# Attention into a soft mixture of experts: score tiles of one head's keys instead of two heads' halves, V single buffered, and a new hand-written order

## The chip, the cores and the metric

The kernel runs on one core of a Trainium2 chip. The core has five engines with a queue of instructions each: PE (matrix products, with weight loads that run ahead of them), DVE (element-wise work), ACT (functions such as tanh and exp), POOL (general work, and here the issue of the casting transfers) and SP (here only the issue of transfers). An engine works through its own queue in order and waits on semaphores for the others; transfers run on 16 DMA engines.

The metric is the device time of one launch in microseconds; the time of a version is the median over its runs. Times of instructions come from one profiled execution.

## The reference

```python
# q, k, v: (8, 12, 448, 64), cap = 30
scores = q @ k^T / sqrt(64)
scores = cap * tanh(scores / cap)
attn   = softmax(scores)                   # over the keys
x      = (attn @ v) as 3584 tokens x 768   # 12 heads side by side

logits = x @ phi                           # 768 x 32: 8 experts, 4 slots each
slots  = softmax(logits over the tokens)^T @ x
h      = relu(slots[e] @ w1[e])            # 768 -> 1024, for each expert
out_s  = h @ w2[e]                         # 1024 -> 768
out    = softmax(logits over the slots) @ out_s
```

Attention is most of the work: 96 heads (8 batches of 12) of 448 queries and 448 keys. The expert part reads 25 MB of `w1` and as much of `w2` in float32, cast to bfloat16 on the way.

## The kernel before

**Tiles.** Four heads make a quad (24 of them), two heads a pair `pr` (48). In a quad, the pair `h` of Q and K is turned by PE (`transp`, L337) so that partition 64 h + d holds dimension d; 128 columns hold 64 keys of each of the pair's two heads, for each of seven column groups `c`. A score tile is one `c` of one pair: 128 partitions (64 keys of head 0 above 64 keys of head 1) by 448 queries. `qk_chunk` (L368) makes three tiles, each from two 64x64 products, and the order of the tiles alternates between the two pairs of a quad (`turn`, L169). There are 336 tiles, 112 chunks, and 56 groups of six tiles.

**Softcap and softmax.** ACT takes tanh of a chunk out of PSUM into float16 (`tanh_chunk`, L380). The exponential of a group is then made either by ACT in one instruction (`exp_chunk`, L392) or by DVE in eight instructions, a bit trick with a cubic polynomial (`poly_exp`, L402, steps at L410 to L419). Sixteen groups go to DVE.

**V products.** `pv_mms` (L422) takes the exponentials as weights, 128 queries at a time, against `vbd`, in which the two heads' V stand block by block: 130 columns, 64 of V and one of ones for each head, with zeros where the other head's keys are. The last 64 queries (the tail) are done as two 64x64 products, one for each head. Reciprocal and product on DVE normalise (L444, L448), PE turns the result for the logits (L485), and per batch there follow logits, slot sums and the turned weights of the tokens.

**Loads.** Q and K come through POOL with a cast to bfloat16 (`load`, L251), each into a buffer that the turn two quads before has released. V comes through SP in float32, into two buffers (`load_v`, L259), and POOL casts it into `vbd` (`vcast`, L351). The weights come through POOL between them (`M` in the order): `w1` stays, 13 of the 16 parts of `w2` are parked in DRAM as bfloat16 and are read back when attention releases its memory (L766 to L772), three as whole parts and ten as halves; three parts stay on chip.

**The order.** The stage is written out by hand in `PROGRAM` (L183): `T` tanh of a chunk, `Q` its scores, `p` one of the eight DVE steps of a group, `E` an ACT exponential, `A`/`B`/`t`/`u` the V products of a pair, `r`/`m` its normalisation, `K`/`J` and `k`/`j` turn and copy of K and Q, `X`/`y`/`x` the turn of the output, `L`/`e`/`S`/`s`/`R`/`c`/`W`/`w` the batch work, `M` a weight load, and `G`, `F`, `N` products without use, which keep PE from idling. Each engine meets its instructions in that order. Six groups' buffers `ex` lie in attention's memory, two more (`guests`) in buffers that later take parts of `w2`, and so do `xf` and `xp`, the working buffers of the DVE steps.

**The end.** The last pair, the logits and the slot sums follow by hand; then layer 1, layer 2 for one half of the columns, the first output tiles, layer 2 for the other half, and the output (11 MB).

Of the kernel before, what the change touches and what calls it, by code (L numbers as in the profile page):

```python
# [9 lines left out]
F32 = mybir.dt.float32  # L10
BF16 = mybir.dt.bfloat16
# [27 lines left out]
def kernel(  # L39
# [28 lines left out]
    KEPT = 1 + NGU  # L68
    WHOLE = 3
    EARLY2 = 2  # L70
# [29 lines left out]
    consts.tile([P, 192], BF16, name="pad")  # L100
# [3 lines left out]
    def unit(shape, dt, name):  # L104
        return wts.tile(shape, dt, name=name, tag="w2u", bufs=KEPT + 2)

# [31 lines left out]
    late = len(w2_parts) - NGU  # L138
    w2_kept = w2_parts[:KEPT - NGU] + w2_parts[late:]
    w2_spilled = [(n0, None) for n0 in w2_parts[KEPT - NGU:KEPT - NGU + WHOLE]]  # L140
    w2_spilled += [(n0, half) for half in range(2) for n0 in w2_parts[KEPT - NGU + WHOLE:late]]

# [10 lines left out]

    att = ExitStack()
    ld = att.enter_context(tc.tile_pool(name="ld", bufs=1))
    homes = {}
    for nm in ("qk0", "ldv0", "ex4", "qk1", "ex2", "ldv1", "vb0", "ex1", "ex3", "vb1", "ex5", "ex0"):
        homes[nm] = att.enter_context(tc.tile_pool(name=nm, bufs=1))
# [3 lines left out]
    ldv = [homes["ldv0"], homes["ldv1"]]  # L162
# [21 lines left out]
T0.2 V0.0 V0.1 V1.0 V1.1 T1 Q2 N1.0 T2.1 p0.0 Q3 N4.0 p0.1 T3 p0.2 K1.1 E1 J1.0 k1 j1 Q4 p0.3 Q5  # L184
T4.3 N4.0 p0.4 M0 T5 Q6 p0.5 J2.0 K2.1 T6.4 Q7 j2 T7 k2 Q8 p0.6 N1.0 T8.6 Q9 J3.1 p3.0 T9 Q10 p0.7
K3.0 M1 T10.0 p3.1 Q11 j3 T11 p3.2 A0.1 k3 B0 E2 p3.3 t0 Q12 u0 Q13 A1.0 r0 p3.4 t1 T12.2 B1 m0 u1
M2 p3.5 T13 Q14 J4.1 T14.7 r1 j4 Q15 m1 T15 p3.6 Q16 A2.1 E4 t2 p7.0 K4.0 F7 p3.7 k4 M3 B2 T16.5
p7.1 Q17 X0.0 p7.2 E5 y0 Q18 u2 G9.18 r2 x0 m2 J5.0 p7.3 A3.1 T17 t3 B3 T18.1 p7.4 u3 Q19 M4 r3
G6.19 j5 E6 m3 p7.5 A4.1 Q20 T19 K5.0 p7.6 t4 B4 T20.3 Q21 p9.0 u4 G7.21 E8 r4 m4 M5 k5 A5.1 p7.7
X1.0 t5 p9.1 Q22 T21 B5 p9.2 y1 u5 T22.4 Q23 r5 m5 x1 T23 Q24 X2.1 y2 T24.6 Q25 x2 p9.3 M6 L0.1 T25  # L190
K6.0 k6 e0 E10 J6.1 p9.4 A6.0 j6 Q26 p9.5 t6 Q27 T26.2 B6 u6 p9.6 K7.1 T27 Q28 M7 E12 r6 k7 Q29 m6
G6.29 p13.0 A7.0 p9.7 J7.1 T28.0 t7 p13.1 B7 u7 E11 Q30 r7 m7 G6.30 j7 S0.0 p13.2 M8 A8.1 T29 s0
p13.3 R0.0 T30.7 Q31 t8 c0 B8 p13.4 T31 u8 A9.0 r8 m8 E14 p13.5 X3.1 B9 t9 Q32 u9 Q33 M9 r9 y3 m9
T32.5 G8.33 x3 p13.6 T33 Q34 J8.0 T34.3 A10.1 j8 p16.0 t10 K8.0 E15 p13.7 Q35 B10 k8 u10 Q36 r10
p16.1 M10 A11.0 T35 p16.2 t11 T36.4 Q37 B11 m10 T37 u11 Q38 r11 m11 K9.1 E17 k9 Q39 p16.3 A12.0 J9.1
M11 B12 j9 T38.6 p16.4 X4.1 y4 T39 x4 Q40 p16.5 X5.1 y5 T40.1 Q41 t12 u12 r12 T41 m12 Q42 x5 K10.0
p16.6 T42.2 L1.1 M12 Q43 e1 E18 k10 S1.1 p16.7 A13.0 p20.0 t13 s1 E19 p20.1 J10.1 B13 j10 u13 p20.2
A14.1 r13 T43 Q44 m13 t14 M13 p20.3 R1.0 T44.7 Q45 B14 p20.4 T45 u14 Q46 r14 c1 m14 T46.0 Q47 K11.0
J11.1 T47 k11 j11 A15.0 E22 p20.5 t15 B15 M14 X6.1 Q48 p20.6 u15 Q49 T48.5 y6 x6 T49 p20.7 A16.1 t16
r15 E21 B16 p24.0 u16 Q50 m15 r16 X7.0 m16 M15 Q51 T50.3 y7 A17.1 x7 p24.1 B17 T51 Q52 p24.2 t17 u17  # L200
J12.0 T52.4 r17 Q53 m17 j12 W0.1 E25 w0 K12.0 A18.1 k12 p24.3 X8.0 M16 y8 Q54 T53 B18 x8 t18 T54.6
p24.4 Q55 u18 J13.0 r18 m18 T55 Q56 L2.1 j13 T56.1 p24.5 Q57 K13.0 e2 E23 S2.1 k13 M17 p24.6 A19.0
t19 T57 p27.0 B19 Q58 s2 p24.7 u19 E26 A20.1 r19 B20 m19 t20 p27.1 R2.0 Q59 c2 T58.0 u20 p27.2 N2.0
r20 M18 T59 m20 Q60 p27.3 A21.1 T60.2 Q61 K14.0 p27.4 T61 Q62 k14 p27.5 T62.7 Q63 B21 T63 J14.0 t21
j14 Q64 E28 p27.6 M19 Q65 X9.0 y9 u21 G6.65 r21 x9 m21 T64.5 A22.0 p27.7 K15.1 T65 p31.0 M20 t22 Q66
k15 E29 p31.1 X10.1 B22 p31.2 y10 u22 Q67 r22 G6.67 x10 T66.3 M21 m22 A23.1 p31.3 T67 J15.0 B23 Q68
j15 E30 t23 u23 p31.4 Q69 A24.0 r23 M22 m23 t24 p31.5 B24 T68.4 u24 X11.1 T69 r24 Q70 m24 y11 x11
N1.0 T70.6 p34.0 Q71 M23 J16.0 E33 L3.1 j16 p31.6 A25.0 B25 t25 p34.1 u25 e3 T71 S3.1 M24 r25 m25
Q72 E32 s3 K16.0 p31.7 A26.1 p34.2 B26 k16 Q73 T72.1 p34.3 M25 t26 u26 X12.0 T73 Q74 r26 y12 x12
T74.0 m26 Q75 A27.0 p34.4 E35 B27 M26 p34.5 t27 u27 Q76 R3.1 r27 G6.76 c3 T75 m27 A28.1 p34.6 W1.0  # L210
t28 T76.7 Q77 M27 w1 p34.7 K17.0 T77 B28 k17 E36 J17.0 p38.0 u28 j17 Q78 r28 p38.1 M28 A29.0 T78.5
m28 B29 p38.2 X13.1 E37 t29 y13 Q79 x13 u29 Q80 r29 K18.1 m29 M29 k18 A30.0 p38.3 T79 X14.1 t30 y14
# [20 lines left out]
    raws, casts, qkT = {}, {}, {}  # L233

    srcs = {"q": q, "k": k, "v": v}

# [9 lines left out]
    def raw_tile(nm):  # L246


        return ld.tile([P, 2, S], BF16, name=nm + "b", tag=nm + "raw", bufs=2)
# [696 lines left out]
```

## Time and profile before

| | |
|---|---|
| median of three runs | 287.5 us (287.15 to 288.88) |
| profiled execution, its own time | 287.71 us |
| its span | 285.8 us |
| busy: PE, weight loads | 235.0 us (82%), 164.4 us (58%) |
| busy: DVE, ACT, POOL | 242.4 us (85%), 248.3 us (87%), 138.8 us (49%) |
| mean granted PE clock | 0.979 of full speed |
| read from and written to HBM | 93.68 MB, 21.23 MB |

How to read the lines below: a page or an answer of the trace names an instruction by its line in the kernel, its engine, and `out<-in` by the program's names. In the groups by shape there follow the count, the busy time, the mean in ns of one, and the engine's idle time just before them with what ended it. "A <- B: 5.0, 7, 1.8" in the waits is a total of 5.0 us in 7 waits, the longest 1.8. In the view of a tile stand the smallest, median and largest duration in ns. In the timeline and the chain, start and duration in us. Matmuls are pipelined: one's duration includes its latency, so many fit into less than the sum.

### The profile page before, as it was taken

The numbers are of one execution on the slowest core, as the hardware profiler recorded it, in microseconds if no ns is written. First come the engines' busy times: TensorE is split into PE (matmuls) and PEld (weight loads), VectorE is DVE, ScalarE is ACT, GpSimd is POOL, SyncE is SP. The second block draws the span as 40 slices with busy tenths as digits, with TensorE's granted clock in tenths as the row PEclk, the third lists the DMA queues.
The fourth block names the chain that finished last, engine by engine and source line by source line (L and its number), as shares of the span: only waits on it lengthen the run. The fifth ranks groups of instructions, "written<-read, shape, count | busy, mean of one in ns | idle before, by whom it ended". The sixth has DMA issues, their size and how long they took to land.

```text
span 285.8 us, 10127 instructions
## 1 busy us (share of the span) xinstructions
PE 235.0 (82%) x4483; PEld 164.4 (58%) x4486; DVE 242.4 (85%) x354; ACT 248.3 (87%) x194; POOL 138.8 (49%) x177
## 2 busy tenths in 40 slices
PE   8778678879898879978998889888898999998610
PEld 6336356557566667745766666665676886643300
DVE  3899999999999899999996999999999974338640
ACT  4889999999999999999997999999999996237520
POOL 8933565483664565554854487657343530200000
PEclk9999999999999999999997999999999999999995
DMA  7999999999999999999999999999997999979995
GB/s 241 216 189 193 189 205 229 237 216 225 228 231 225 219 224 239 232 224 218 221 235 206 186 158 212 217 223 210 207 191 161 213 374 409 411 286 379 413 422 226
DMA packets 48987, 69.58 MB, mean 243 GB/s; under 512 B 3760, under 2 KB 38704, under 8 KB 48944
## 3 DMA queue, kind: packets, MB, share of 16 engines
q0 software_dynamic: 33424, 35.77, 75.8%
q1 hardware_dynamic: 15232, 32.94, 32.1%
q8 instruction: 35, 0.57, 0.7%
q10 hardware_dynamic: 288, 0.23, 0.2%
q14 instruction: 8, 0.07, 0.1%
HBM read 93.68 MB, written 21.23 MB: 402 GB/s over the span
## 4 chain that ended last, share of the span: by engine, by line
DVE 39%; PE 26%; ACT 21%; DMA 4%; issue 4%; POOL 1%; DVEq 0%; ACTq 0%; POOLq 0%
ACT ex L386 11%; PE pv L436 8%; PE sc L377 4%; DVE xq L448 4%; DVE xp L416 4%; ACT ex L390 4%; DVE ex L417 4%; DVE xp L414 4%; DVE xp L413 3%; DVE qT L347 3%; DVE xf L412 2%; ACT exg L390 2%; DMA w2d<-in_moe_w_dram 2%; DVE xp L415 2%; DVE kT L347 2%
## 5 line engine op out<-in xcount | busy, mean ns | idle before, releaser
L386 ACT ACTIVATE ex<-sc 128x1344 f16<-128x1344 f32 (+1 forms) x89 | 110.9, 1319 | 5.1 <-PE sc L377 5.0
L436 PE MATMUL pv<-vbd,ex 128*128 128x130 bf16 (+1 forms) x1285 | 81.9, 211 | 11.4 <-DVE xT L505 3.5
L436 PEld LDWEIGHTS <-ex 128*128 128x128 bf16 (+1 forms) x1320 | 65.4, 102 | 26.2 <-issue 5.3
L390 ACT ACTIVATE ex<-ex 128x2688 bf16<-128x2688 f16 x31 | 77.1, 2497 | 0.0
L354 POOL CAST vbd<-vraw 64x896 bf16<-64x896 f32 x48 | 57.8, 1205 | 33.7 <-issue 31.6
L377 PE MATMUL sc<-qT,kT 64*64 64x448 bf16 x672 | 65.3, 361 | 9.6 <-ACT ex L386 4.1
L377 PEld LDWEIGHTS <-kT 64*64 64x64 bf16 x672 | 22.6, 105 | 21.2 <-issue 12.2
L436 PE MATMUL pv<-vbd,exg 128*128 128x130 bf16 (+1 forms) x360 | 29.9, 213 | 1.6 <-DVE xq L448 1.4
L386 ACT ACTIVATE exg<-sc 128x1344 f16<-128x1344 f32 x24 | 30.5, 1323 | 0.5 <-PE sc L377 0.5
L448 DVE TENSOR_TENSOR xq<-pv,rec 128x448 bf16<-128x448 f32 x47 | 29.1, 619 | 0.9
L254 POOL DMA_DIRECT2D kb<-in_k_dram x22 | 16.4, 744 | 21.9 <-PE kps L342 21.6
L416 DVE TENSOR_TENSOR xp<-xp,xf 128x2688 f16<-128x2688 f16 x16 | 25.7, 1609 | 0.1
L254 POOL DMA_DIRECT2D qb<-in_q_dram x22 | 16.7, 758 | 17.9 <-PE qps L342 17.1
L414 DVE TENSOR_TENSOR xp<-xp,xf 128x2688 f16<-128x2688 f16 x16 | 24.8, 1551 | 0.0
L436 PEld LDWEIGHTS <-exg 128*128 128x128 bf16 (+1 forms) x360 | 20.8, 102 | 6.6 <-issue 2.4
L390 ACT ACTIVATE exg<-exg 128x2688 bf16<-128x2688 f16 x8 | 19.8, 2480 | 0.0
L417 DVE TENSOR_TENSOR ex<-ex,xp 128x2688 uint16<-128x2688 uint16 x12 | 18.6, 1550 | 0.1
L134 POOL DMA_DIRECT2D w2d<-in_moe_w_dram x20 | 16.5, 833 | 0.3 <-issue 0.3
L413 DVE TENSOR_SCALAR xp<-xf 128x2688 f16<-128x2688 uint16 x16 | 16.2, 1016 | 0.2
L361 POOL MEMSET vbd<- 64x1 bf16 x22 | 5.8, 264 | 21.7 <-PE pv L436 21.4
L505 DVE COPY xT<-xps 128x896 bf16<-128x896 bf16 (+1 forms) x24 | 14.2, 592 | 1.7 <-PE xps L496 1.0
L347 DVE COPY kT<-kps 128x896 bf16<-128x896 bf16 x23 | 14.2, 616 | 1.6 <-PE kps L342 1.6
(133 smaller groups left out, 358.9 us busy)
## 6 DMA issues: line engine op xcount, KB each, us to landing
w1b<-in_moe_w_dram POOLq DMA_DIRECT2D x16, 768.0 KB, 10.9
vraw<-in_v_dram SPq DMA_DIRECT2D x44, 224.0 KB, 6.4
w2d<-in_moe_w_dram POOLq DMA_DIRECT2D x20, 384.0 KB, 8.5
w2t<-w2d SPq DMA_DIRECT2D x20, 384.0 KB, 7.7
out_dram<-ob SPq DMA_DIRECT2D x7, 768.0 KB, 8.6
qb<-in_q_dram POOLq DMA_DIRECT2D x22, 224.0 KB, 8.3
kb<-in_k_dram POOLq DMA_DIRECT2D x22, 224.0 KB, 8.0
out_dram<-obh SPq DMA_DIRECT2D x9, 384.0 KB, 3.4
```

The source lines that it names most:

```text
L254: pool.dma_start(out=t, in_=quad_ap(nm, Q))
L347: dve.tensor_copy(qkT[nm, Q], held.pop((nm, Q)))
L354: pool.tensor_copy(vbds[Q % 2][r, :, :, c0:c0 + DH], raw[r])
L377: pe.matmul(sc[cs, u, 0:S], qkT["k", Q][r, c, cs], qkT["q", Q][r, :, cs], start=True, stop=True)
L386: act.activation(exs[j][:, half * CS + u0:half * CS + u1, :].bitcast(F16), sc[:, u0:u1, 0:S], ACT.Tanh, scale=qk_scale / cap)
L390: act.activation(exs[j][:, u0:u1, :], exs[j][:, u0:u1, :].bitcast(F16), ACT.Exp, scale=cap)
L413: lambda: dve.tensor_scalar(p, f, c3, c2, ALU.mult, ALU.add),
L414: lambda: dve.tensor_tensor(p, p, f, op=ALU.mult),
L416: lambda: dve.tensor_tensor(p, p, f, op=ALU.mult),
L417: lambda: dve.tensor_tensor(y, y, p, op=ALU.add),
L436: pe.matmul(out_, exs[j][r, u, q0:q0 + (HP if tail else P)], v_, start=(c == 0 and g == gs[0] < NF), stop=(c == NT - 1), skip_group_check= ...
L448: dve.tensor_tensor(xq[Q][:, h, s0:s1, :], pv[:, 0:s1 - s0, 0:DH], recs.pop(pr).to_broadcast([P, s1 - s0, DH]), op=ALU.mult)
```

## The change

**Keys.** The turned K of a pair is stored by head. In `kT` the columns now hold, for each head, three column groups of 128 keys, and the seventh group's 64 keys of one head, beside 64 columns of zeros, make the mixed tile. A score tile `c` > 0 has 128 keys of one head and is one 64x128 product; tile 0 has 64 keys of each head and is two products that add up in the same place, each with zeros in the other head's half. (Which of the mixed tile's rows belongs to which head is settled by the zeros.)

```diff
-            for n in range(2):
-                cs = slice(n * HP, n * HP + HP)
-                pe.matmul(sc[cs, u, 0:S], qkT["k", Q][r, c, cs],
-                          qkT["q", Q][r, :, cs], start=True, stop=True)
+            for n in range(2) if c == 0 else ((c - 1) % 2,):
+                at = (CS + n if c == 0 else (c - 1) // 2 + n * (CS + 2)) * P
+                pe.matmul(sc[:, u, 0:S], qkT["k", Q][r, at:at + P],
+                          qkT["q", Q][r, :, n * HP:n * HP + HP], start=(c > 0 or n == 0),
+                          stop=(c > 0 or n == 1))
```

**V products.** `vbd` holds 65 columns for each unit of keys. A tile of one head is multiplied by 65 columns; only the mixed tile by 130. The tail of a tile is one product of 64 queries by 65 columns (two for the mixed tile).

```diff
-                    for n in range(2 if tail else 1):
-                        r = slice(n * HP, n * HP + HP) if tail else slice(0, P)
-                        q0, s0 = g * P, 2 * (g - gs[0])
-                        out_, v_ = (dst[r, s0, :], vbds[Q % 2][r, h, c, n * W:n * W + W]) \
-                            if tail else (dst[:, s0:s0 + 2, :], vbds[Q % 2][:, h, c, :])
-                        pe.matmul(out_, exs[j][r, u, q0:q0 + (HP if tail else P)], v_,
+                    q0, s0 = g * P, 2 * (g - gs[0])
+                    for n in (range(2) if tail else (None,)) if c == 0 else ((c - 1) % 2,):
+                        v_ = vbds[Q % 2][:, h, CS:CS + 2, :] if n is None else \
+                            vbds[Q % 2][:, h, CS + n if c == 0 else (c - 1) // 2 + n * (CS + 2), :]
+                        if tail:
+                            out_ = dst[n * HP:n * HP + HP, s0, :]
+                        else:
+                            out_ = dst[:, s0:s0 + 2, :] if n is None else dst[:, s0 + n, :]
+                        pe.matmul(out_, exs[j][:, u, q0:q0 + (HP if tail else P)], v_,
```

**V's path.** One buffer instead of two. A pair of a quad is loaded by four transfers (two heads, two stretches of columns, so that the halves of the partitions hold different keys), and cast by POOL in three instructions; the load of the next quad's pair follows the cast. The memset of one V row that POOL ran once a quad is gone. The last quad's V goes into the released raw buffers of Q and K.

```diff
-    def vcast(Q, n):
-        raw = raws["v", Q].rearrange("p h (c d) -> p h c d", d=DH)
-        r, c0 = slice(n * HP, n * HP + HP), n * W
-        pool.tensor_copy(vbds[Q % 2][r, :, :, c0:c0 + DH], raw[r])
-        load_v(Q + 2, n)
+    def vcast(Q, h):
+        raw, t = v_raw(Q, h), vbds[Q % 2]
+        pool.tensor_copy(part(t[:, h, :, :], 0, [(CS + 2) * W, 2], [W, CS], [1, DH]),
+                         part(raw, 0, [(CS + 1) * DH, 2], [DH, CS], [1, DH]))
+        for n in range(2):
+            r = slice(n * HP, n * HP + HP)
+            pool.tensor_copy(t[r, h, CS + n, 0:DH], raw[r, CS * DH:(CS + 1) * DH])
+        if Q < NQ - 2:
+            load_v(Q + 1, h)
...
-        if h == 0 and 1 < Q + 1 < NQ:
-            pool.memset(vbds[Q % 2][HP:P, h, NT - 1, 0:1], 0.0)
-            vcast(Q + 1, 1)
-        elif h == 1 and Q + 2 < NQ:
-            vcast(Q + 2, 0)
+        if Q + 2 < NQ:
+            vcast(Q + 2, h)
```

**Parked parts.** Six buffers instead of five for parts of `w2`, two of them free from the start; three parts are kept as before. Of the 13 parked ones six are whole (before three) and seven halved (before ten). Two half parts are read back into the raw buffers of Q and K, one of them (`O` in the order) before the stage ends.

```diff
+    def reload_raw(n):
+        t = rawt[:, 2 - 2 * n:4 - 2 * n, :].rearrange("p n s -> p (n s)")
+        reload(WHOLE + n, t[:, 0:4 * HD].rearrange("p (n d) -> p n d", d=HD))
...
-    for n in (0, *range(WHOLE, WHOLE + EARLY2), *range(1, WHOLE), *range(WHOLE + EARLY2, len(w2_spilled))):
+    for n in (0, WHOLE + 2, WHOLE + 3, 1, 2, 3, WHOLE + 1, *range(4, WHOLE), *range(WHOLE + 4, len(w2_spilled))):
+        if n == WHOLE + 1:
+            reload_raw(1)
+            continue
```

**The start.** The first piece of K has four column groups instead of three; the second half of the first turn comes between the scores of chunk 0 and chunk 1, and two products without use between them are gone.

```diff
     first_half(0)
     qk_chunk(0)
+    first_half(1)
     qk_chunk(1)
-    spare(2)
-    first_half(1)
```

**The order.** `PROGRAM` is new throughout: 17 groups go to DVE (136 `p` in place of 128) and one fewer to ACT (38 `E` in place of 39, the last group apart); there are 39 weight loads in place of 42; the products without use in score banks are 241 in place of 66 (`G`), those in V banks 32 in place of 21 (`F`), and the wide ones 19 in place of 13 (`N`).

More of the change, by code (lines that the diff above doesn't have):

```diff
@@ L189 @@
[L189 to L194, printed above, removed]
@@ L205 @@
[L205 to L210, printed above, removed]
@@ L233, with part, k_unit @@
     raws, casts, qkT = {}, {}, {}
+    kTs = [qk[n].tile([P, (NT + 1) * P], BF16, name=f"kT{n}") for n in range(2)]
+    def part(x, off, *dims):
+        return bass.AP(tensor=x.tensor, offset=x.offset + off, ap=[x.ap[0]] + [list(d) for d in dims])
+    KS = (NT + 2) * HP
+    def k_unit(c):
+        return (2 * c if c <= CS else 2 * (c - CS - 1) + 1) * HP
     srcs = {"q": q, "k": k, "v": v}
```

209 lines of the change are left out of this document (125 added, 84 removed).

## The prediction

> **What bounds the kernel now.** I read four views in this order: the shares of the chain of waits (which engines it ran through), busy time by stretch (how full each engine is in each stage), the chain in order of time near its end (what hands over to what), and the groups by shape (prices).
>
> ```profile
> span 285.8 us, 10127 instructions
> DVE 39%; PE 26%; ACT 21%; DMA 4%; issue 4%; POOL 1%; DVEq 0%; ACTq 0%; POOLq 0%
> ```
>
> ```profile
> 10.00:230.00 220.00, 189.08 (x3791) 136.58 (x3792) 212.05 (x295) 216.00 (x152) 125.86 (x151) 0.99 1.14 213
> 150.00:160.00 10.00, 8.56 (x142) 6.46 (x140) 7.79 (x12) 8.18 (x6) 4.75 (x7) 0.83 1.25 212
> 254.00:285.80 31.80, 14.86 (x137) 6.06 (x133) 15.65 (x24) 13.50 (x20) 0.00 (x0) 0.87 0.88 347
> ```
>
> ```profile
> 198.19 2.33 ACT exg L390
> ...
> 232.36 4.26 PE pv L436 x93
> ...
> 239.06 1.65 PE pvl L436 x35
> ```
>
> The columns of the second view are stretch, length, then PE, weight loads, DVE, ACT and POOL busy, granted clock, DMA share, GB/s. The attention stage runs to about 242 us. From 10 to 230 us ACT is busy 216.0 of 220 and DVE 212.05, so 4.0 and 8.0 us are idle; PE idles 31. Two engines are nearly full, and the third feeds both. The chain therefore changes hands: DVE early, ACT back to back from about 190 us (one exponential of six tiles adds 2.33 us there), and at the end PE with V products, because nothing else is left to do. After 254 us it is stores. So PE time saved in the middle is worth only the waits that PE causes, while PE time saved in the last 10 us is worth its full price, and what ACT and DVE have to do counts almost in full.
>
> **Scores.** Before, a tile takes two 64x64 products, and three tiles six of them.
>
> ```profile
> 140.63 0.56 PE L377 MATMUL sc<-qT,kT 64*64 64x448 bf16 x6
> L377 PE MATMUL sc<-qT,kT 64*64 64x448 bf16 x672 | 65.3, 361 | 9.6 <-ACT ex L386 4.1 <-DVE qT L347 2.6 <-ACT exg L386 1.1
> ```
>
> Six matmuls of 361 ns each fit in 0.56 us, so several run side by side. After, one 64x128 product does a whole tile, with the two pairs' rows still in different halves of the array. I expect the same 0.56 us for three tiles with half the instructions. The trace has no 64x128 product; a gain is excluded up to the point where three products run together (361 against 560 ns, 0.07 us a tile, 22 us for 336 tiles) and a loss goes to one after another (3 x 0.36 = 1.08 us, +58 us of PE). I take no change, the nearest row being the same streams in four quarters. The mixed tile costs a second product: 48 more, two pairs side by side, 24 x 0.19 (a third of 0.56) = 4.6 us more PE, between 0 and 48 x 0.36 = 17.
>
> **V products.** Of the 1008 wide ones, 144 (mixed tiles) stay at 130 columns and 864 go to 65.
>
> ```profile
> 160.23 0.86 PE L436 MATMUL pv<-vbd,ex 128*128 128x130 bf16 x12 [0.48 <-DVE ET L548]
> 145.94 0.61 PE L510 MATMUL lps<-phib,xT 128*128 128x32 bf16 x18
> ```
>
> Both are runs of one matmul per new 128x128 weight. Twelve of 130 columns take 0.86 us, eighteen of 32 columns 0.61: 72 and 34 ns each. A straight line between them gives 47 ns for 65 columns, 25 ns less, so 864 x 25 = 22 us of PE time; bounds 0 (weights set the pace) and 864 x 38 = 33. [...]
>
> The tails go from two half products side by side to one of 64 columns per tile; I leave them unchanged. Against this stand longer runs of idle-time products: 241 instead of 66 narrow ones in score banks, which sit where PE would wait. In sum PE loses some 10 us, from 189 to about 180 of 220: not the bound before, and less so after. What it is worth is in the waits:
>
> ```profile
> ACT ex L386 <- PE sc L377: 5.0, 7, 1.8
> DVE rec L444 <- PE pv L436: 3.8, 8, 1.1
> DVE kT L347 <- PE kps L342: 1.6, 3, 0.7
> ```
>
> **The division between ACT and DVE.** The new order has 17 groups in eight DVE steps instead of 16, and one exponential less on ACT: -2.3 us there by the chain's row. The group's price on DVE is the sum of eight rows:
>
> ```profile
> L410 DVE TENSOR_SCALAR ex<-ex 128x2688 uint16<-128x2688 f16 x12 | 11.2, 931 | 0.1
> L412 DVE TENSOR_SCALAR xf<-ex 128x2688 uint16<-128x2688 uint16 x12 | 12.4, 1034 | 0.0
> L413 DVE TENSOR_SCALAR xp<-xf 128x2688 f16<-128x2688 uint16 x16 | 16.2, 1016 | 0.2
> L414 DVE TENSOR_TENSOR xp<-xp,xf 128x2688 f16<-128x2688 f16 x16 | 24.8, 1551 | 0.0
> L415 DVE TENSOR_SCALAR xp<-xp 128x2688 f16<-128x2688 f16 x16 | 14.4, 898 | 0.1
> L416 DVE TENSOR_TENSOR xp<-xp,xf 128x2688 f16<-128x2688 f16 x16 | 25.7, 1609 | 0.1
> L417 DVE TENSOR_TENSOR ex<-ex,xp 128x2688 uint16<-128x2688 uint16 x12 | 18.6, 1550 | 0.1
> L418 DVE TENSOR_SCALAR ex<-ex 128x2688 uint16<-128x2688 uint16 x12 | 10.7, 894 | 0.0
> ```
>
> That is 9.48 us, say +9.5. DVE had only 8.0 us idle, so the group fits only if DVE's other time shrinks. One thing can shrink it:
>
> ```profile
> L412 DVE TENSOR_SCALAR xf<-ex x12: 841/870/1572, 11.0 to 221.3; 128x2688 uint16<-128x2688 uint16 x12
> L413 DVE TENSOR_SCALAR xp<-xf x16: 840/890/1492, 12.5 to 222.1; 128x2688 f16<-128x2688 uint16 x16
> 11.01 1.47 DVE L412 TENSOR_SCALAR xf<-ex 128x2688 uint16<-128x2688 uint16 x1
> 8.32 4.97 POOL L354 CAST vbd<-vraw 64x896 bf16<-64x896 f32 x4
> ```
>
> These steps take 0.84 us when nothing disturbs them and 1.47 while POOL casts V (8.32 to 13.29 us). The five one-input steps take 4.77 us on average against 5 x 0.84 = 4.20, and L416 0.06 more than its twin L414: 0.63 us a group, 10.1 us over 16 groups, is what POOL costs DVE here. POOL's casts change:
>
> ```profile
> L354 POOL CAST vbd<-vraw 64x896 bf16<-64x896 f32 x48 | 57.8, 1205 | 33.7 <-issue 31.6 <-POOL vbd L354 0.4
> L361 POOL MEMSET vbd<- 64x1 bf16 x22 | 5.8, 264 | 21.7 <-PE pv L436 21.4
> L354 POOL CAST vbd<-vraw x48: 921/990/2359, 8.3 to 233.4; 64x896 bf16<-64x896 f32 x48
> L361 POOL MEMSET vbd<- x22: 94/97/778, 36.2 to 233.2; 64x1 bf16 x22
> ```
>
> Before, 48 casts of 896 elements and 22 memsets take 63.6 us. After, each cast is one of 384 elements on all partitions and two of 64. By the medians an element costs (990 - 97) / 895 = 1.0 ns over a fixed 0.1, so 0.48 + 2 x 0.16 = 0.80 us, 48 of them 38 us, 40% less, in pieces a third as long. I take 6 of the 10.1 us as won back, because a short piece also blocks for less time; bounds 0 and 10. Of DVE's 8.0 idle us I take 5.5 as closed (5.4 of the waits above are for PE, and the stretch 150 to 160 us alone holds 2.2); bounds 0 and 8.
>
> **The start.** Chunk 1 of the scores moves behind the second half of the first turn.
>
> ```profile
> 9.52 0.56 PE L377 MATMUL sc<-qT,kT 64*64 64x448 bf16 x4 [0.56 <-DVE qT L312]
> 10.12 2.47 ACT L386 ACTIVATE ex<-sc 128x1344 f16<-128x1344 f32 x2 [1.09 <-PE sc L377]
> ```
>
> The first turn's second half now comes earlier on PE, so the copies that held PE 0.56 and ACT 1.09 us come earlier too: ACT -0.9, first DVE step -0.4 (0 if the casts hold it). The longer first K piece (4 of 7 columns instead of 3) costs under 0.1.
>
> **V single buffered.** A load waits for the cast of the quad before, and is due a quad later, about 220 / 24 = 9.2 us.
>
> ```profile
> vraw<-in_v_dram SPq DMA_DIRECT2D x44, 224.0 KB, 6.4
> L264 SPq DMA_DIRECT2D vraw<-in_v_dram x44: 595/595/709, 9.3 to 221.3; - x44
> ```
>
> Landing takes 6.4 us and the four smaller transfers add three issues, 1.8 us: 8.2 of 9.2 us. What hides it is that the cast runs two quads ahead of its use; if late, it first stalls POOL, behind which Q, K and weight loads queue. I cost it at nothing; if the cover goes, the bound is a microsecond a quad.
>
> **Reloads and end.** The same 13 parts are reloaded, but one half part (0.39 MB) goes into raw buffers before the stage ends, one into raw buffers after.
>
> ```profile
> 230.84 16.52 SPq L771 DMA_DIRECT2D w2t<-w2d  x18
> 230.00:242.00 12.00, 11.27 (x208) 8.80 (x205) 7.43 (x19) 10.49 (x10) 2.24 (x3) 1.00 1.00 396
> 254.14 11.65 SPq L838 DMA_DIRECT2D out_dram<-obh  x15
> ```
>
> At 396 GB/s 0.39 MB is 1.0 us less behind the last DVE group. The first store leaves at 254.14; it waits for the end of attention, and the reload ends about then too, so both must move for the stores to move. Bigger whole parts come due earlier, since six instead of three are needed whole by the first half of layer 2; I cost that at nothing, as no row of the waits has layer 2 waiting for a reload.
>
> **Sum.** ACT: -2.3 (exponential), -1.5 of its 5.0 us of waits for scores, -0.9 (start) = -4.7. DVE: +9.5 - 0.4 - 6 - 5.5 = -2.4 at its last group; behind that the 93 V products of 4.26 us at the end, 46 ns each, shrink by about 30%, -1.3: -3.7. The later of the two decides, -3.7, and the reload (-2.4 - 1.0) goes along. The profiled run took 287.7 us (span 285.8 and 1.9 around it), so 284.0; the median of three runs is 0.2 lower, so **283.8 us**.
>
> **Rivals.**
> *ACT decides alone* (B): DVE has room, ACT closes 3.5 of its 5.0 us: -6.7, 280.8. For: the chain's ACT stretch from 190 us. Against: DVE's 8 us of room are what the new group needs.
> *Contention falls only as POOL's time does* (C): 4 of 10.1 us and 5 of the gaps: DVE +0.1, -1.3 behind it, 286.3. For: the price in proportion is the plainest reading. Also the outcome if reloads hold back the stores by 2 us.
> *DVE becomes the bound* (D, slower): the disturbance comes from POOL's issue of loads rather than from the casts, nothing is won back and half the gaps stay: +9.5 - 0.4 - 4 = +5.1, -1.3: +3.8, 291.3. It decides from the point where contention and gaps together give back less than 7.8 us (9.5 - 0.4 - 1.3). For: DVE holds 39% of the chain. Against: the 1.47 us step under the casts.
> *The PE clock falls more often* (E, slower):
>
> ```profile
> 151.17:154.58 3.41, 3.41 (x39) 3.04 (x42) 2.73 (x3) 2.08 (x2) 1.48 (x2) 0.50 1.21 211
> ```
>
> Once PE ran 3.41 us at half its clock, and in the 10 us around it DVE lost 2.2 us. A PE with 10 us less to do pauses more; four more such dips cost 8.8 us: -3.7 + 8.8 = +5.1, 292.6. The third decides. Against: the added idle-time products. [...]
> That the change doesn't do what it says I leave out: the order of instructions has fewer PE rows and 17 groups.
>
> **Chances.** Forecast 0.42 (own range 282.2 to 284.6), B 0.13, C 0.25, D 0.13, E 0.07. What a measurement can tell from no change is 1%, 284.6 and 290.4 us. Faster: 0.42 + 0.13 = 0.55; within: 0.25; slower: 0.20. The range from 280.0 to 290.5 takes in B and C and leaves out D and E, 0.20 together.
>
> **What would show it.** Right: one exponential less and 136 eight-step rows; one-input DVE steps near 0.9 us on average; V casts under 0.5 and 0.2 us; a run of 65-column products near 47 ns each; attention's last scores' exponential some 4 us earlier; first store near 250.5. Wrong: three tiles of scores over 0.6 us; DVE's busy time up by more than 5 us with its steps still near 0.95; granted clock under 0.95 in more than one stretch; layer 2 waiting for a reload; POOL waiting for V.

## The result, and the profile after

The changed kernel takes 298.3 us (median of four runs, 295.4 to 299.7), the kernel before 287.3 (four runs): a ratio of 1.037 (95% interval 1.027 to 1.046). A ratio, here and below, is taken from the runs that lie within 1.5% of their kernel's fastest, so it can differ a little from the ratio of the medians. The prediction was 283.8 us in a range of 280.0 to 290.5. It was wrong: the time is above the range, and the sign is the other one. The profiled execution is the fastest of the four, 295.4 us with a span of 293.5.

The page of the changed kernel: span, shares of the chain, and the granted clock in 40 slices of 7.3 us.

```profile
span 293.5 us, 9705 instructions
...
DVE 39%; PE 23%; ACT 19%; DMA 9%; issue 3%; POOL 1%; SPq 1%; DVEq 0%; POOLq 0%; ACTq 0%
...
PEclk9999999669999999999999999956999999999975
```

Transfers now stand in the chain with 9% (4% before), and the clock stood at half twice during attention, for 10.2 and 13.7 us (3.4 us once before). Busy time by stretch, with the columns of the prediction's second view:

```profile
10.00:230.00 220.00, 186.78 (x3295) 120.29 (x3297) 207.80 (x295) 208.40 (x147) 146.92 (x212) 0.95 1.13 207
150.00:160.00 10.00, 9.20 (x192) 5.89 (x189) 9.84 (x15) 10.00 (x8) 8.81 (x14) 1.00 0.75 132
180.00:190.00 10.00, 6.17 (x151) 4.58 (x150) 8.34 (x13) 7.93 (x5) 9.79 (x16) 0.98 1.03 163
190.00:200.00 10.00, 9.28 (x75) 4.53 (x76) 6.62 (x10) 7.16 (x5) 5.75 (x11) 0.50 1.27 219
```

From 10 to 230 us ACT is busy 208.4 us and DVE 207.8, where it was 216.0 and 212.05: both wait more, and not everywhere, but in a few stretches, such as 180 to 200 us. The transfers slow down in 180 to 190 us too (163 GB/s), and already in 150 to 160 us (132 GB/s), where ACT and DVE are still full; in both stretches POOL is nearly full. What is late is seen in the waits, first of the engines, then of SP's queue:

```profile
POOL vbd L401 <- DMA vraw<-in_v_dram: 35.3, 17, 3.5
PE qps L383 <- DMA raws<-in_q_dram: 4.0, 2, 3.7
ACT ex L436 <- PE sc L426: 8.0, 7, 4.5
```

```profile
SPq L291 <- POOL vbd L405: 105.5, 43, 7.0
```

POOL waits 35.3 us for V to land, a wait that the same answer for the kernel before doesn't list; PE waits for Q; ACT waits for PE, 4.5 us at one time. SP waits for POOL's casts before it may load V again (182.4 us in 44 waits before, when it had a quad to spare). The timeline of POOL, and one row of PE's, show one such round:

```profile
170.00 0.75 POOL L401 CAST vbd<-vraw 128x384 bf16<-128x384 f32 x1 [1.87 <-DMA vraw<-in_v_dram]
...
173.72 0.51 POOL L401 CAST vbd<-vraw 128x384 bf16<-128x384 f32 x1 [2.49 <-DMA vraw<-in_v_dram]
...
182.58 0.73 POOL L274 DMA_DIRECT2D raws<-in_q_dram  x1
```

```profile
190.25 0.96 PE L383 MATMUL qps<-ident,raws 128*64 128x128 bf16 x14 [3.71 <-DMA raws<-in_q_dram]
```

POOL stands before a cast, and the loads behind it in its queue leave late and close together. The Q load issued at 182.58 us landed at 190.21, where PE had stood for 3.7 us and the clock had just gone to half. The chain of waits of this profile runs through just these steps, twice through V's load and cast, then through the Q load behind them:

```profile
168.30 5.27 DMA vraw<-in_v_dram
...
173.72 0.51 POOL vbd L401
...
177.60 4.27 DMA vraw<-in_v_dram
...
182.58 7.63 DMA raws<-in_q_dram
```

The end, in the timelines of ACT and SP, first before, then after:

```profile
237.30 2.63 ACT L686 ACTIVATE ex<-ex 128x1536 bf16<-128x1536 f16 x3
```

```profile
222.26 0.96 SPq L771 DMA_DIRECT2D w2t<-w2d_None  x1
```

```profile
242.64 2.63 ACT L740 ACTIVATE ex<-ex 128x1536 bf16<-128x1536 f16 x3
```

```profile
229.51 0.40 SPq L159 DMA_DIRECT2D raws<-w2d  x1
...
261.15 12.32 SPq L891 DMA_DIRECT2D out_dram<-obh  x15
```

The last exponential is 5.3 us later, the first reload of parked weights 7.3, the first store 7.0 (254.14 before). From there both kernels take about 32 us to the end. So of the 7.7 us between the two profiled spans 5.3 are made in the attention stage. Another 1.7 come between the last exponential and the first store; the reloads are late there, but the trace lists no wait of PE for one, so their part in it is not shown.

### The profile page after: what moved, and what is told of

It reads as the page before. It is cut to its first block, busy times and chain, and to the rows that moved or that the text cites. A ratio compares the mean times of both kernels' runs of the same rounds, so it can differ in the third digit from the quotient of the medians.

```text
span 293.5 us, 9705 instructions
## 1 busy us (share of the span) xinstructions
PE 239.5 (82%) x4097; PEld 151.4 (52%) x4100; DVE 244.2 (83%) x362; ACT 246.3 (84%) x193; POOL 164.0 (56%) x254
## 4 chain that ended last, share of the span: by engine, by line
DVE 39%; PE 23%; ACT 19%; DMA 9%; issue 3%; POOL 1%; SPq 1%; DVEq 0%; POOLq 0%; ACTq 0%
ACT ex L436 8%; PE pv L489 6%; ACT ex L440 6%; PE sc L426 5%; DVE xp L464 4%; DVE xp L466 4%; DVE xq L501 4%; DMA raws<-in_q_dram 4%; DMA vraw<-in_v_dram 3%; DVE ex L467 3%; DVE xf L462 3%; DVE xp L465 3%; DVE xp L463 3%; DVE kT L392 2%; ACT exg L440 2%
## 5 line engine op out<-in xcount | busy, mean ns | idle before, releaser
L436 ACT ACTIVATE ex<-sc 128x1344 f16<-128x1344 f32 x86 | 107.0, 1335 | 10.7 <-PE sc L426 8.0
L426 PE MATMUL sc<-qT,kT 64*128 64x448 bf16 x384 | 70.2, 368 | 8.3 <-ACT ex L436 4.7
L401 POOL CAST vbd<-vraw 128x384 bf16<-128x384 f32 x46 | 37.3, 811 | 68.7 <-DMA vraw<-in_v_dram 35.3
L489 PE MATMUL pv<-vbd,ex 128*128 128x65 bf16 (+2 forms) x1042 | 57.3, 205 | 6.0 <-POOL vbd L405 2.8
L489 PEld LDWEIGHTS <-ex 128*128 128x128 bf16 (+1 forms) x1071 | 44.5, 104 | 25.7 <-issue 10.8
L405 POOL CAST vbd<-vraw 64x64 bf16<-64x64 f32 x92 | 50.4, 547 | 2.8
L436 ACT ACTIVATE exg<-sc 128x1344 f16<-128x1344 f32 (+2 forms) x27 | 33.3, 1281 | 2.1 <-PE sc L426 2.1
L383 PEld LDWEIGHTS <-raws 128*64 128x64 bf16 x616 | 20.9, 113 | 22.0 <-issue 13.3
L426 PEld LDWEIGHTS <-kT 64*128 64x128 bf16 x384 | 18.5, 95 | 24.6 <-issue 12.3
L466 DVE TENSOR_TENSOR xp<-xp,xf 128x2688 f16<-128x2688 f16 x17 | 26.9, 1581 | 0.0
L489 PE MATMUL pv<-vbd,exg 128*128 128x65 bf16 (+2 forms) x321 | 21.1, 202 | 3.6 <-DVE exg L468 1.5
```

What stands on the lines that cost most here:

```text
L383: pe.transpose(dst, src[:, h, c * DH:(c + 1) * DH], ident)
L401: pool.tensor_copy(part(t[:, h, :, :], 0, [(CS + 2) * W, 2], [W, CS], [1, DH]), part(raw, 0, [(CS + 1) * DH, 2], [DH, CS], [1, DH]))
L405: pool.tensor_copy(t[r, h, CS + n, 0:DH], raw[r, CS * DH:(CS + 1) * DH])
L426: pe.matmul(sc[:, u, 0:S], qkT["k", Q][r, at:at + P], qkT["q", Q][r, :, n * HP:n * HP + HP], start=(c > 0 or n == 0), stop=(c > 0 or n == 1))
L436: act.activation(exs[j][:, half * CS + u0:half * CS + u1, :].bitcast(F16), sc[:, u0:u1, 0:S], ACT.Tanh, scale=qk_scale / cap)
L466: lambda: dve.tensor_tensor(p, p, f, op=ALU.mult),
```

## The experiments

Three theories stood at the start. A: V's single buffer makes POOL wait, the loads behind it go out late, and PE, ACT and DVE starve. B: the three casts a pair are what is dear, whatever the buffers. C: the new order, with 17 groups on DVE, is at fault. The texts put down before each run, printed below, call POOL GpSimd. In the table, "median" is over all runs of a kernel, and the ratio is to the kernel before on the same chip.

| run | median, us | ratio (95%) |
|---|---|---|
| after, two V buffers, one w2 part less kept | 286.9 | 0.997 (0.993 to 1.001) |
| after, one w2 part less kept | 296.6 | 1.031 (1.025 to 1.037) |
| before, one V buffer | 291.6 | 1.015 (1.007 to 1.023) |
| after, no 64x64 casts | 290.2 | 1.005 (1.001 to 1.010) |
| after, ring of three V halves | 289.2 | 1.003 (0.999 to 1.007) |
| ring, one group back to ACT | 292.4 | 1.017 (1.012 to 1.021) |
| ring, no 64x64 casts | 291.8 | 1.002 (0.998 to 1.006) |
| after, fill before one Q turn | 297.8 | 1.032 (1.026 to 1.039) |
| two V buffers, PE kept busy | 287.2 | 0.998 (0.994 to 1.002) |
| after, PE kept busy | 297.9 | 1.034 (1.028 to 1.040) |
| ring, PE kept busy | 286.8 | 0.995 (0.992 to 0.999) |
| after, two transfers a half | 293.9 | 1.019 (1.014 to 1.024) |
| before, one V buffer, four transfers | 299.1 | 1.039 (1.034 to 1.044) |
| the same, buffers in place | 298.6 | 1.041 (1.032 to 1.050) |
| before, one V buffer, buffers in place | 290.7 | 1.013 (1.007 to 1.020) |
| before, two V buffers, four transfers | 287.8 | 1.000 (0.996 to 1.005) |

### Is it the V buffer?

Two buffers in the changed kernel:

```diff
-    NFREE = 2
+    NFREE = 1
...
-    vraw = homes["ldv"].tile([P, 2, S], F32, name="vraw")
+    vraws = [homes["ldv"].tile([P, 2, S], F32, name=f"vraw{n}") for n in range(2)]
...
-        if Q < NQ - 2:
-            load_v(Q + 1, h)
+        load_v(Q + 2, h)
```

> The changed kernel with two V buffers again: the load of a quad's V is issued two quads ahead of its cast, as before. The room (3.5 KB a partition) comes from keeping one w2 part less on the chip, so one more part (0.79 MB) is parked and read back at the end; at the 396 GB/s of the stretch 230 to 242 us before, that may cost up to 2 us. Theory A (V single buffered: GpSimd waits 35 us for V to land, the K, Q and weight loads behind it go out late, PE waits for them and its clock halves): the waits for V vanish, the granted clock is back above 0.96, and the time falls from 298.3 to 286 to 290. Theory B (the three casts a pair are what is dear, 88 us of GpSimd for 64, wherever V lands): 294 to 299. Theory C (the new order with its 17 DVE groups is at fault): 296 to 300, DVE and ACT still starving at the same places.

Its control, with only the first of these edits:

> The control of the run with two V buffers: the changed kernel with one w2 part less kept on the chip, V single buffered. All theories: 298 to 301, as the changed kernel plus up to 2 us for the part that is read back. If it is much slower, the two-buffer run is to be read against this one.

The pair of runs differs by the second buffer (which the last quad's V then uses too): 296.6 against 286.9 us, 9.7 us. Theory A's time came, the others' didn't; the clock that it named, above 0.96, came in part (0.950 to 0.980). The control was expected at 298 to 301 us and lies below that, so the part that is read back costs nothing that these runs show. In the control's profile V's path stands in the chain with 24% for its loads, 7% for their issues (L291) and 7% for the casts (L401 and L405):

```profile
DMA vraw<-in_v_dram 24%; ACT ex L436 8%; SPq L291 7%; DMA raws<-in_q_dram 7%; DMA w2t<-w2d 6%; ACT ex L440 5%; POOL vbd L401 4%; PE sc L426 3%; DMA w2t<-w2d_None 3%; POOL vbd L405 3%; PE pv L489 3%; DMA out_dram<-ob 2%; ACT exg L440 2%; PE op L903 2%; ACT exg L436 1%
```

With two buffers V's loads hold 2% of the chain. Of that run, a wait, the stretch, ACT's last exponential and the first store:

```profile
POOL vbd L400 <- DMA vraw<-in_v_dram: 3.0, 1, 3.0
```

```profile
10.00:230.00 220.00, 187.59 (x3472) 122.47 (x3475) 215.94 (x308) 217.20 (x154) 149.87 (x223) 1.00 1.18 224
```

```profile
233.59 2.63 ACT L738 ACTIVATE ex<-ex 128x1536 bf16<-128x1536 f16 x3
```

```profile
250.02 12.95 SPq L889 DMA_DIRECT2D out_dram<-obh  x15
```

The waits for V go from 35.3 to 3.0 us, ACT and DVE are full again (217.2 and 215.9 of 220), and the stage ends 3.7 us earlier than before instead of 5.3 later.

The other way round, one buffer in the kernel before:

```diff
-    vraw = [ldv[n].tile([P, 2, S], F32, name=f"vraw{n}") for n in range(2)]
+    vraw = [ldv[0].tile([P, 2, S], F32, name="vraw0")] * 2
...
-        load_v(Q + 2, n)
+        load_v(Q + 1, n)
```

> The kernel before with one V buffer: the same two transfers a quad, each issued only after the cast of the quad before it. Tiles, order, casts and groups stay those of before. Theory A: GpSimd now waits for V here too (6.4 us from issue to landing, in 9.2 us a quad), the loads behind it are late, 291 to 298. Theories B and C: the single buffer is covered and the time stays within 1% of 287.3.

291.6 us: the low edge of what A gave, and 4 us, not 10. So the single buffer costs here too, but something in the changed kernel makes it cost more.

Without the small casts:

```diff
-        for n in range(2):
+        for n in range(2 if Q < 2 else 0):
             r = slice(n * HP, n * HP + HP)
             pool.tensor_copy(t[r, h, CS + n, 0:DH], raw[r, CS * DH:(CS + 1) * DH])
```

> The changed kernel without the two 64x64 casts of a pair from the third quad on: the mixed tile's V of those quads is left out (the buffer holds that of an earlier quad). 50 us of GpSimd go, and 1.1 us of each pair's round from V's landing to its next load. Theory A: part of the loss comes back, since the round of load, landing and cast gets 1.1 us of room a pair, 289 to 295, with GpSimd still waiting for V. Theory B: all of the loss that the casts make comes back, 284 to 288. Theory C: 296 to 299.

290.2 us, inside A's range and above B's: part of the loss comes back, and POOL still waits 55.6 us for V, so this is again the round of load and cast, now shorter.

### What is left once V has room

A ring of three halves (a half is the V of one pair of a quad), with no more weights parked for it:

```diff
-    vraw = homes["ldv"].tile([P, 2, S], F32, name="vraw")
+    vraws = [homes["ldv"].tile([P, S], F32, name=f"vraw{n}") for n in range(3)]
...
-        if Q < NQ - 2:
-            load_v(Q + 1, h)
+        load_v(*divmod(2 * Q + h + 3, 2))
```

> The changed kernel with its V buffer grown from two halves (one quad) to a ring of three: a half's load is issued one and a half quads ahead of its cast, about 13.8 us, instead of one, 9.2 us. The room is found without parking anything more: the 512 ones for the idle-time products become 128 (each such product is split into four), and the reciprocals lie in the unused end of a DVE scratch buffer. Theory A (V's round of load, landing and cast has no slack): 284 to 287, that is 9 us or more below the changed kernel and, without the extra part of the two-buffer run (286.9), at or a little below it; granted clock 0.96 or more. Theory B (the casts themselves, and how GpSimd's pieces fall) and theory C (the order): not below 288.

Ratio 1.003: most of the loss comes back, less than A's number said (284 to 287). Its twelve runs lie between 285.1 us, at a mean granted clock of 0.980, and 291.9; the five slowest have clocks of 0.932 to 0.953, so something that shows in the clock was left. Two kernels on top of it, one with group 34 as an ACT exponential, one without the small casts:

```diff
-p34.0
...
-p34.3
+E34
...
-p34.7
```

> The kernel with the ring of three halves, but group 34 goes from eight DVE steps back to one exponential on ACT, so DVE has 16 groups, as before the change. If ACT and DVE are level, as the forecast's sum has it, ACT's 2.33 us come on top: 1 to 2.5 us slower than the ring with 17 groups. If DVE had become the bound (the forecast's rival D): 2 us or more faster, since 9.1 us of DVE work go.

> The kernel with the ring of three halves, without the two 64x64 casts of a pair from the third quad on (the mixed tile's V of those quads is left out). Theory A: with V early enough, GpSimd's dear casts have cover, and 46 us of them less gain under 1%, 282 to 286.5. Theory B in the weaker form that the casts still cost DVE and the loads something: 3 us or more below the ring kernel.

The group back on ACT costs 1.4% (1.017 against 1.003), 4 us, more than the 1 to 2.5 that I had put: DVE is not the bound, and theory C falls. The small casts, some 43 us of POOL, are worth nothing once V is early (1.002 against 1.003): B falls too. A's number for this run, 282 to 286.5, did not come either; its twelve runs spread from 285.9 to 296.1 us.

### The clock

Sixteen fill products in front of the Q turn at which PE had stood for 3.7 us:

```diff
-p41.5 J20.0 T89
+p41.5 N16.0 J20.0 T89
```

> The changed kernel with 16 idle-time products of 512 columns (some 0.2 to 0.4 us each) in front of the Q transposes of quad 20, where PE waited 3.7 us for Q until 190.25 us and where its clock then stood at half until 203. V stays single buffered. If the half clock is what makes late loads dear: no drop near 190, and 3 to 4 us less, 294 to 295.5. If the waits themselves are what costs: the drop goes, but the time stays 297 to 299.5, since the transposes still wait for Q.

The time stays at 297.8 us, as the second theory had it. The clock row of its page, and the stretch in which the changed kernel's clock had stood at half:

```profile
PEclk9999999995799985999999999999999999999965
```

```profile
189.60:203.25 13.65, 12.25 (x156) 7.18 (x158) 10.29 (x16) 9.95 (x8) 10.48 (x18) 1.00 1.25 206
```

At full clock, ACT is still busy only 9.95 of 13.65 us there, and drops come at two other places. More such edits, at five places, in three kernels:

```diff
-K6.0 Q23
+Q23 G10.23 K6.0
...
-J6.0 E9 Q25 x2
+Q25 G14.25 J6.0 E9 x2
...
-u8 J8.1
+u8 G16.30 J8.1
...
-J12.1 E24 Q53
+Q53 G12.53 J12.1 E24
...
-p34.5 J17.0
+p34.5 G12.76 J17.0
```

> The kernel with two V buffers, and PE kept busy at five places where it paused 0.7 to 1.4 us in most profiles so far (the transposes of K6, Q6, Q8, Q12 and Q17): score chunks 23, 25 and 53 move ahead of these transposes, and 64 narrow idle-time products go in front of them. In the profiles so far the granted clock halves right after a stretch of 3.41 us in which PE was busy for less than some two thirds. If these halvings are what still separates the runs of one kernel (284.8 to 289.9 us with two buffers): the runs draw together near 284 to 286, granted clock 0.97 or more. If they are only a sign of other waits: no change, 286 to 288. If the fill stands in the way of scores: slower, 288 to 290.

> The changed kernel with the same five edits and the 16 products ahead of Q20's transposes; V stays single buffered. If most of the loss was the half clock (24 us of it in the profile): 290 to 294. If the late loads cost by the waits themselves: 295 to 299, whatever the clock does.

> The kernel with the ring of three V halves and the same five edits. If the clock explains the spread of the ring kernel (285.1 to 291.9 us): 284.5 to 287, closer together, granted clock above 0.965. If not: 288 to 290.

With V single buffered the time stays (297.9), although the mean granted clock rises in most runs: 0.955 or more in three of five, against 0.934 to 0.944 in the changed kernel. The run at 0.968 took 297.3 us; by an estimate from its mean it had some 19 us at half clock, where the records of the changed kernel's profile have 38 and those of the kernel before 14 (10 us of each at the very end). With two buffers the time stays too (287.2), and the runs don't draw together (284.9 to 291.3). With the ring the ratio falls by 0.7% (0.995 against 1.003), and that kernel is the only one whose interval lies below 1. But its twelve runs spread from 285.3 to 293.1 us and don't draw together either; their mean, 288.3, is no lower than the 287.9 of the kernel before. Two rows of its profile, the clock and ACT's last exponential:

```profile
PEclk9999999999999999999999999999999999999965
```

```profile
232.04 2.63 ACT L741 ACTIVATE ex<-ex 128x1536 bf16<-128x1536 f16 x3
```

So the half clock goes with the late loads and isn't what makes the 11 us: with most of it gone, in one run, the time is the same, where it was kept up ACT starved as well, and the mirror run below is as slow at a mean granted clock of 0.953 to 0.961. Whether the fill helps the ring kernel at all, and why it doesn't help the one with two buffers, stays open.

### Why 10 us here and 4 in the kernel before

The load of a quad's V can't leave before the cast of the quad before it is done, and the next cast can't begin before the load has landed. From the records of the transfers, as medians over 44 loads of a half, this round is in the changed kernel: 7.8 us from the first issue to the last landing, 0.2 to the cast, 1.9 for the three casts, less 0.3 that the first issue is ahead of the last cast: 9.7 us before rounding (the expectations below, from a first reading, say 9.3). Its casts of the same half follow each other at 9.8 us, 28 of 44 of them within 0.5 us of the landing, so V's round paces POOL for much of the stage; in the kernel before they follow each other at 9.1, the length of a quad. With one buffer and one transfer a half there the same medians give 6.0 + 0.2 + 1.0 = 7.2. If this length decides, it can be moved in both kernels. Two transfers a half in the changed kernel, and four in the other:

```diff
...
+            if Q < NQ - 1:
+                n4 = (CS + 1) * DH
+                for r0, at, step in ((0, 0, S * DH + CS * DH), (HP, n4, S * DH - n4)):
+                    sp.dma_start(out=vraw[r0:r0 + HP, h, :].rearrange("p (g x) -> p g x", g=2),
+                                 in_=bass.AP(tensor=src.tensor, offset=src.offset + 2 * h * S * DH + at,
+                                             ap=[[NT * DH, HP], [step, 2], [1, n4]]))
...
```

```diff
-            sp.dma_start(out=vraw[Q % 2][r],
...
+            for h in range(2):
+                for c0, c1 in ((0, 4 * DH), (4 * DH, S)):
+                    sp.dma_start(out=vraw[Q % 2][r, h, c0:c1],
...
```

> The changed kernel, V single buffered, but a half's V comes in two transfers instead of four (up to the last quad; each brings 4 units of two heads, one of them unused, so 14% more bytes of V). In the changed kernel's trace V's round takes some 9.3 us a quad: 8.0 from the first issue to the last landing, of which 2.4 are four issues, 0.2 to the cast, 1.9 for the three casts, less 0.8 overlap. A quad takes 9.1 us. If the length of this round against the quad is what decides: 1.2 us less round, GpSimd's waits for V fall from 35 us to under half, and the time to 289 to 294. If it is the lead of one quad as such: 296 to 299.

> The mirror of it: the kernel before with one V buffer (291.6 us so far, its round 6.25 + 0.2 + 1.0 = 7.5 us of 9.1), with each half's V in four transfers instead of one. If the length of the round decides: 1.8 us more, 9.3, no slack, and 295 to 299, near the changed kernel although nothing else of the change is in it. If not: 291 to 293.

Both times came: 293.9 us, 4 less, and 299.1 us, 7.5 more, as slow as the changed kernel without anything else of it. The first did not come by the step that I had put, though. Its transfers and waits:

```profile
vraw<-in_v_dram SPq DMA_DIRECT2D x92, 128.0 KB, 6.2
```

```profile
POOL vbd L408 <- DMA vraw<-in_v_dram: 34.0, 16, 5.6
```

The larger transfers take 6.2 us to land instead of 5.5. From the first issue to the last landing it is 7.5 us where it was 7.8, the casts take 2.1 us where they took 1.9, and the same sum of medians gives 9.6: the round is shorter by 0.1 us, not 1.2, and POOL's waits stay. Where the 4 us come from is not shown; the buffer is also a seventh larger, which moves others.

The mirror run had moved the buffers behind the second V buffer, and its first reload left 15 us later than before. Three more kept every buffer in its place (the second one is reserved and not used):

```diff
-    vraw = [ldv[0].tile([P, 2, S], F32, name="vraw0")] * 2
+    vraw = [ldv[n].tile([P, 2, S], F32, name=f"vraw{n}") for n in range(2)][:1] * 2
```

> The kernel before with one V buffer in four transfers a half, as in the run of 299.1 us, but the second buffer's room stays reserved, so that no other buffer moves. In that run the first reload of parked w2 left at 237.2 us instead of 222.3, since it lands in a buffer that lay elsewhere and came free later; part of its loss is this. If the length of V's round decides in the attention stage too: the stage ends 2 to 4 us later than before (239.9 us) and the time is 290 to 294. If all of that run's loss was the place of the buffers: 287 to 289.

> The kernel before with one V buffer in one transfer a half, the room of the second one reserved. Its round of 7.5 us fits into a quad: 287 to 289, the 291.6 us of the first such run being the buffers' place. If the single buffer itself costs: 290 to 293.

> The kernel before with its two V buffers, but four transfers a half: the number of transfers alone. Two quads of lead cover it: 286.5 to 289. If the added issues and smaller pieces cost by themselves (descriptors, SP's queue): 290 or more.

The place is not it: 298.6 with it kept (more than the 290 to 294 that I had put). The number of transfers alone is not it: 287.8 with two buffers. The single buffer alone is 290.7. Only both together, the single buffer and a longer load, make the whole loss. Rows of the kernel before with one buffer in four transfers:

```profile
POOL vbd L355 <- DMA vraw<-in_v_dram: 49.8, 25, 5.6
```

```profile
242.55 2.63 ACT L687 ACTIVATE ex<-ex 128x1536 bf16<-128x1536 f16 x3
```

```profile
239.31 0.35 SPq L772 DMA_DIRECT2D w2t<-w2d_None  x1
```

and of the same with one transfer a half, whose round fits:

```profile
POOL vbd L353 <- DMA vraw<-in_v_dram: 14.1, 10, 4.5
```

```profile
235.72 2.63 ACT L685 ACTIVATE ex<-ex 128x1536 bf16<-128x1536 f16 x3
```

```profile
225.81 0.35 SPq L770 DMA_DIRECT2D w2t<-w2d_None  x1
...
234.40 16.91 SPq L770 DMA_DIRECT2D w2t<-w2d  x18
```

```profile
PE so_ps L820 <- DMA w2t<-w2d: 3.3, 4, 1.2
```

With four transfers the round is 7.9 + 0.3 + 1.0 = 9.2 us by the same medians, the casts follow each other at 9.8 as in the changed kernel, and the stage ends at 242.55, as late as the changed kernel's 242.64; V's loads hold 20% of that profile's chain. The sum is hardly more than a quad's 9.1: a round with no room left seems to be enough, since the casts wait for PE as well (7.1 us for scores and 7.0 for V products there). With 7.2 the stage ends even before 237.30, and the 3 us that this kernel loses come later: the reloads stand on SP's queue behind the last loads of V, and layer 2 waits 3.3 us for them, a wait that the kernel before doesn't list. It isn't the first reload that decides. That one leaves at 225.81 instead of 222.26 (239.31 with four transfers), but with two buffers in four transfers it is as late, at no loss; what differs there is the run of 18 behind it:

```profile
225.26 0.35 SPq L773 DMA_DIRECT2D w2t<-w2d_None  x1
...
231.15 17.24 SPq L773 DMA_DIRECT2D w2t<-w2d  x18
```

That is a second price of the single buffer in the kernel before. In the changed kernel, whose first reload is 7.3 us late, layer 2 lists no wait for one.

## Why the prediction was wrong

**The step that failed** is "V single buffered", which I cost at nothing. It had the round at 8.2 of 9.2 us, 6.4 for landing and 1.8 for three more issues, and took the cast's lead of two quads over its use as the cover. Two things were wrong with that. The sum left out the casts, which are part of the round: with them and the real landings it is 9.7 us, more than a quad. (With the 0.80 us that I had put for the casts elsewhere it would have been 9.0 and still have fitted; it takes the 1.9 that they measured.) And the lead covers the wrong thing. It held: by the records, V is cast 12 us ahead of its first product in the median of the 48 pairs, where it was 8 in the kernel before, and PE hardly waits for it:

```profile
PE pv L489 <- POOL vbd L405: 3.5, 5, 1.0
```

What it doesn't cover is POOL itself, which stands 35.3 us in front of its casts while Q, K and weight loads wait behind them in its queue; PE then waits for Q, and ACT for PE. V was hardly late for its products; the queue was late for everything else. This was named in the same step (POOL stalls, and Q, K and weight loads queue behind it), and its bound, "a microsecond a quad", would have held the loss; I gave it no place among the rivals. Of the signs of being wrong that I had listed, two showed: POOL waiting for V, and a clock under 0.95 in more than one stretch.

**The casts** were the mis-sized term behind it: 0.80 us a pair by a straight line through sizes, 38 us in all.

```profile
L405 POOL CAST vbd<-vraw 64x64 bf16<-64x64 f32 x92 | 50.4, 547 | 2.8
L401 POOL CAST vbd<-vraw 128x384 bf16<-128x384 f32 x46 | 37.3, 811 | 68.7 <-DMA vraw<-in_v_dram 35.3 <-PE pv L489 12.2 <-PE qps L383 7.7
```

```profile
L405 POOL CAST vbd<-vraw x92: 229/235/1597, 8.5 to 232.4; 64x64 bf16<-64x64 f32 x92
L401 POOL CAST vbd<-vraw x46: 499/662/1796, 8.1 to 231.1; 128x384 bf16<-128x384 f32 x46
```

They take 1.90 us a pair, 88 us in all. Their shortest durations are near the line (0.50 + 2 x 0.23 = 0.96 us); the other 0.94 us looks like waiting for DVE. In the records of the changed kernel 59 of the 92 small casts take 0.23 to 0.24 us and the other 33 take 0.75 to 1.60, and each of these 33 ends 0.09 to 0.10 us after one of a group's steps on DVE (L460 to L468) has ended. The long cast of before took 1.20 us in the mean for 0.92 at the shortest, 0.28 more. Why a cast waits there is not shown; that three short casts pay such a wait up to three times, where one long cast paid it once, is my reading of 0.94 against 0.28 us.

**The other steps**, from the profiles of the changed kernel (its PE and DVE groups) and of the one with two buffers:

```profile
L426 PE MATMUL sc<-qT,kT 64*128 64x448 bf16 x384 | 70.2, 368 | 8.3 <-ACT ex L436 4.7 <-ACT exg L436 1.4 <-DVE kT L392 1.3
L489 PE MATMUL pv<-vbd,ex 128*128 128x65 bf16 x639 | 33.2, 198 | 0.8 <-issue 0.7
```

```profile
L466 DVE TENSOR_TENSOR xp<-xp,xf 128x2688 f16<-128x2688 f16 x17 | 26.9, 1581 | 0.0
...
L463 DVE TENSOR_SCALAR xp<-xf 128x2688 f16<-128x2688 uint16 x17 | 14.9, 875 | 0.1
```

*Scores*: 70.2 us of PE against 65.3, +4.9 for an estimate of 4.6; but the changed kernel ran 24 us of the stage at half clock, and with two buffers, at full clock, it is 66.7, +1.4. *V products*: 33.2 us for 639, 52 ns each, for an estimate of 47; the tails, which I had left unchanged, fell by 10 us (36.8 to 27.0). *Contention*: the step at L463 went from 1016 to 875 ns, L466 from 1609 to 1581, and the eight rows' means together from 9.48 to 9.11 us; over 17 groups that is 6.3 us won back for an estimate of 6. That the number fits is at least in part luck: it was to come from 40% less time of POOL's casts, and that time went up, from 63.6 us with the memsets to 93; leaving the small casts out of the ring kernel didn't lower the eight rows either (9.12 to 9.23 us). Whether the shorter pieces did it, the other reason given, no run separates. *The stage*: with two buffers its last exponential starts 3.7 us earlier, for a sum of -3.7, and the first store leaves at 250.02 for 250.5. So the stage without the failed step came out as forecast, and the profiled run of that kernel, the fastest of ten, took 284.8 us for a forecast of 283.8. Its median is higher, 286.9 against 288.0 of the kernel before beside it, a ratio of 0.997 that is not clear of no change.

**The rivals.** D (DVE the bound) is refuted by the group put back, on the ring kernel. E (the clock) came in part: four more drops were its price, and the changed kernel has two that last 24 us together, but E put them down to PE having less to do, and with most of them gone the time stayed. None of the four rivals decided.

## What to carry to other kernels

Before taking a buffer away, add up the whole round that then becomes serial: issue of every piece, landing, the reader's own time with its waits, and the hand back, and compare it with the period, with room left for the reader's other waits; a lead of the data over its use says nothing of the queue that waits for it. Then list what stands behind both waiting instructions in their queues, here loads of Q and K behind a cast, and reloads behind V; putting those loads ahead of the cast was not tried. If there is room for half a buffer more, that may be enough: three halves instead of two brought back most of the loss (289.2 us, and 286.8 with PE kept busy, where the kernel before had 287.7 both times).

## What the runs showed of the hardware

The drops of the clock during attention, three in the profiles of the two kernels, lasted 3.41 us before and 10.24 and 13.65 in the changed kernel, once, three and four times 3.41; the last two, at 53.07 and 189.60 us, start 40 times that apart. Ahead of each, PE was busy for only a part of 3.41 us. In the changed kernel, each time the stretch ahead and the drop itself; then one of the kernel before that was followed by a drop, and one of the run with two buffers that was not:

```profile
49.65:53.07 3.42, 1.93 (x42) 1.29 (x38) 3.42 (x5) 3.42 (x3) 3.31 (x6) 1.00 1.01 169
53.07:63.31 10.24, 10.24 (x183) 7.52 (x180) 7.89 (x13) 8.63 (x8) 4.54 (x9) 0.50 1.15 213
186.19:189.60 3.41, 0.35 (x9) 0.18 (x5) 2.19 (x4) 1.74 (x2) 3.30 (x8) 1.00 1.22 186
189.60:203.25 13.65, 12.53 (x111) 6.57 (x111) 8.49 (x13) 8.44 (x6) 7.17 (x15) 0.50 1.27 216
```

```profile
147.75:151.17 3.42, 2.29 (x76) 1.59 (x75) 3.31 (x7) 3.42 (x4) 1.75 (x2) 1.00 1.25 229
```

```profile
64.29:67.70 3.41, 2.07 (x30) 1.05 (x27) 3.41 (x5) 2.36 (x3) 3.30 (x4) 1.00 1.14 217
```

PE was busy 1.93, 0.35 and 2.29 us of 3.41 ahead of the drops, and 2.07 where none came, so busy time alone doesn't settle it. PE was busy all through the drop of 10.24 us. What sets the length of a drop, and what ends it, is not shown.
